# A gated linear recurrence and a feed-forward network: first product in three one-pass products of 12-bit parts, second product plain, one written order for the whole kernel

## The chip, the cores and the metric

The kernel runs on one core of one Trainium2 chip. The metric is the device time of one execution in microseconds (us); the median of several runs is compared. A core has a matrix engine (TensorE, PE in the profile, with its weight loads shown as PEld), VectorE (DVE), ScalarE (ACT), GpSimd (POOL) and a synchronising engine (SP). SP, POOL and ACT also issue DMA transfers. Each engine executes its own instructions in order; between engines semaphores decide who waits.

## The reference, cut to what matters

Float32 throughout. B = 4 batches, H = 8 heads, S = 768 steps, D = 48; 3072 tokens with 384 features; the hidden layer has 2048.

```python
scale = np.minimum(mag, 0.999) / (mag + 1e-06)          # mag = |a_re + i a_im|
for t in range(S):                                      # complex state, one D x D matrix per head
    new_re = ar * S_re - ai * S_im
    new_im = ar * S_im + ai * S_re
    S_re, S_im = (new_re + kv, new_im)                  # kv = outer(k[t], v[t])
    y[:, :, t] = np.einsum('bhd,bhde->bhe', q[:, :, t], S_re)
...
x = attn_out.transpose(0, 2, 1, 3).reshape(B * S, H * D)
h = x @ w_in                                            # (3072 x 384) @ (384 x 2048)
g = h * (1.0 / (1.0 + np.exp(-h)))
return g @ w_out                                        # (3072 x 2048) @ (2048 x 384)
```

## The kernel before

**Tiling.** The 768 steps of a batch are six chunks of 128. The 24 chunks (n = 0 to 23) are taken in 12 pairs (p = 0 to 11), a pair being the same chunk of two batches, so that the feed-forward network sees 256 tokens at a time. Per chunk the recurrence becomes a masked attention: logarithms and angles of the gates (`gates_...`, ACT and DVE), their running sums by a triangular matrix on PE (`phases`, `sums`, line 446 with the operand in two parts of type float32r), sines and cosines (`trig`), decayed and rotated keys and queries (`rotated`, line 540), transposition (`turned`: on PE for n < 4, otherwise 32 x 32 blocks on DVE and twelve DMAs, line 571), scores (`weights`, line 584), mask (`masked`, line 595), output (`output`, lines 614 and 617; lines 651 and 654 for n < 4) and state (`state`, lines 674 and 687). The output is copied to `xT` (line 623, or `put`, line 662, for n < 4).

**Feed-forward network.** Each pair has eight groups jp of 256 hidden units. `hidden` (line 725) makes h for one group: 2 x 3 float32 products of 128 x 128 weights with 256 tokens. `silu` (line 733) applies the activation, PSUM to SBUF. `result` (line 763) multiplies g by `w2`: for p = 0 and 1 plainly, four products of 384 columns per group (line 773); from p = 2 on (`WINO = 2`) by `result_of_halves` (line 790), a scheme with seven products of half size instead of eight (line 817, 192 columns, two hidden blocks at once, so seven per group). That scheme needs sums of the g quarters (`sums_of`, line 760, four DVE operations per group), sums of the weights (`combined`, line 748), and a final step of one ACT copy (line 825) and seven DVE additions (line 829).

**Weights.** The weights arrive as 64-bit floats. `fetch` loads 28 blocks as raw pairs of words (line 191), `high_part` and `convert_low` (lines 47, 49, 224) and `joined` (line 56) turn them into float32 on DVE and ACT, straight into `w1` and `w2`. At the end small pieces of the weights are loaded again and looked at (`small`, line 250, `looked_at`, line 257), which guards a slow path that is not taken here.

**What sets the order.** Pairs 0 to 2 follow a list of tokens written by hand (lines 1020 to 1042); each token is a call, and each engine gets its instructions in the order of the list. In it `h:0` is the first group of `hidden`, `m:..` a mask, `x:0` and `x:1` the copies to `xT` that `h:0` reads. `warm` puts idle matmuls in (line 951). From pair 3 on `step` follows one string (`usual`, lines 1048 and 1049): attention of pair p between the `h` and `r` groups of pair p - 1. Pools rotate their buffers; `kr`, `qr`, `sq`, `part`, `xT`, `y3` (one) and `carry` mostly have two. The DMAs of SP and POOL are issued where the token stands.

Of the kernel before, what the change touches and what calls it, by code (L numbers as in the profile page):

```python
# [30 lines left out]
L_MIN = -60.0  # L31
# [26 lines left out]

@with_exitstack
def kernel(  # L60
# [38 lines left out]
    WINO = 2  # L99
# [5 lines left out]
    ld = fast.enter_context(tc.tile_pool(name="ld", bufs=2))  # L105
    pre = fast.enter_context(tc.tile_pool(name="pre", bufs=1))
    att = fast.enter_context(tc.tile_pool(name="att", bufs=2))
    moe = fast.enter_context(tc.tile_pool(name="moe", bufs=2))
    setup = ExitStack()
    su = setup.enter_context(tc.tile_pool(name="su", bufs=1))  # L110
    conversion = ExitStack()
    cv = conversion.enter_context(tc.tile_pool(name="cv", bufs=1, side="right"))
    later = {}
    startup_psum = ExitStack()
    p_m = fast.enter_context(tc.tile_pool(name="p_m", bufs=2, space=PSUM))
    p_h = fast.enter_context(tc.tile_pool(name="p_h", bufs=2, space=PSUM))
    p_o = startup_psum.enter_context(tc.tile_pool(name="p_o", bufs=4, space=PSUM))
# [20 lines left out]
    def load_a(p, queue=None):  # L138
        for name in ("re", "im"):
            A[p][name] = flat(pre.tile([C, 2, H, D], F32, tag=name, name=f"{name}{p}", bufs=2))  # L140
        for i in range(2):
            b, c = place(2 * p + i)
            for name, ap in (("re", a_re), ("im", a_im)):
                (queue or (nc.gpsimd if p == 0 and i and name == "re" else nc.sync)).dma_start(
                    out=cut(A[p][name], i).rearrange("p (h d) -> p h d", d=D),
                    in_=ap[b].rearrange("h (c p) d -> p c h d", p=C)[:, c])

    def load_x(n, names="kqv", queue=None):
        b, c = place(n)
        for name, ap in zip("kqv", (k, q, v)):  # L150
            if name not in names:
                continue
            if name == "v":

                X[n]["all v"] = ld.tile([C, DM + 64 - D], F32, tag="v", name=f"v{n}", bufs=4)
                nc.gpsimd.memset(X[n]["all v"][:, DM:], 0.0)
                X[n]["v"] = X[n]["all v"][:, 0:DM].rearrange("p (h d) -> p h d", d=D)
            else:
                X[n][name] = ld.tile([C, H, D], F32, tag=name, name=f"{name}{n}", bufs=2)
            (queue or nc.sync).dma_start(  # L160
                out=X[n][name], in_=ap[b].rearrange("h (c p) d -> p c h d", p=C)[:, c])
# [5 lines left out]
    w1 = consts.tile([C, ND, DF], F32)  # L167
# [6 lines left out]
    for s in range(DF // WC):  # L174
        for dc in range(ND):
            blocks.append((w1[:, dc, ts(s, WC)], (1, s), [
                (at, w_in[r:r + n, ts(s, WC)]) for at, r, n in rows_in(H, D, ND, dc)]))
        for j in range(s * WC // C, (s + 1) * WC // C):
            blocks.append((w2[:, j], (2, j // 2), [(0, w_out[ts(j, C)])]))
# [24 lines left out]
    def words(n):  # L204
        if n == len(fetched):
            fetch(1)
        dst, _, parts = blocks[n]
        return dst, fetched[n], parts[0][1].dtype != F32

    def convert_high(n):  # L210
        for _ in range(min(n, len(blocks) - len(highs))):
            dst, raw, does = words(len(highs))
            if does:
                high_part(nc, dst, raw[:, :, 1])
            highs.append(dst)

    def convert_low(n):

        for _ in range(n):
            dst, raw, does = words(len(lows))  # L220
            r = None
            if does:
                r = cv.tile([C, WC], I32, tag="wr", name="r", bufs=3)[:, 0:dst.shape[1]]
                nc.scalar.mul(r, raw[:, :, 0].bitcast(U32), 2.0 ** -29)
            lows.append(r)

    def convert(n):

        for _ in range(min(n, len(blocks) - len(done))):
            if len(done) == len(lows):  # L230
                convert_low(1)
            if len(done) == len(highs):
                convert_high(1)
            dst, r = highs[len(done)], lows[len(done)]
            if r is not None:
                joined(nc, dst, r)
            done.append(dst)

    def converted(which):
        while any(x[1] == which for x in blocks[len(done):]):  # L240
            convert(1)
# [32 lines left out]
    load_a(0)  # L274
# [10 lines left out]
    chained = []  # L285
    by_hand = []
    looks, looked = [], []

    def behind(ins, other):
        tc.add_manual_dep(ins.ins, other.ins.name, mybir.DependencyInfo(  # L290
            mybir.DependencyClass.NoSync, mybir.DependencyReason.DATA))

    def chain(ins):
        if chained and not by_hand:
            behind(ins, chained[-1])
        chained.append(ins)


    def table(of):
        chain(nc.scalar.preload_act_table_set({  # L300
            "exp": "natural_log_exp_and_others", "trig": "trig_and_small",
            "silu": "silu_and_others"}[of]))

    def special(out, in_, func, **kw):
        chain(nc.scalar.activation(out=out, in_=in_, func=func, **kw))  # L305


    def tiles(p, i):

        g = A[p]  # L310
        if "th" not in g:
            for x in ("s1", "s2", "mag"):
                g[x] = flat(pre.tile([C, 2, H, D], F32, tag="t3", name=f"{x}{p}", bufs=5))
            for x in ("l", "th"):
                pool = su if p == 1 else pre
                g[x] = flat(pool.tile([C, 2, H, D], F32, tag=x, name=f"{x}{p}"))
        names = ("re", "im", "s1", "s2", "mag", "l", "th")
        return (g[x] if i is None else cut(g[x], i) for x in names)
# [5 lines left out]
    def squares(p):  # L324
        re, im, s1, s2, _, _, th = tiles(p, None)
# [4 lines left out]
    def gates_square(p):  # L330

        squares(p)
        magnitude(p)

    def magnitude(p):
        re, im, s1, s2, *_ = tiles(p, None)
# [3 lines left out]
    def gates_log(p):  # L340

        re, im, s1, s2, mag, *_ = tiles(p, None)
        special(s1, s1, AF.Ln)
        special(mag, s1, AF.Exp, scale=0.5)
        gates_excess(p)

    def gates_excess(p):
        re, im, s1, s2, *_ = tiles(p, None)
# [3 lines left out]

    def gates_inverse(p):

        re, im, s1, s2, mag, _, th = tiles(p, None)
        nc.vector.tensor_tensor(out=mag, in0=mag, in1=th, op=ALU.add)
        special(mag, mag, AF.Ln)
        special(mag, mag, AF.Exp, scale=-1.0)


    def early_square(i):
        re, im, s1, s2, _, _, th = tiles(0, i)
        special(s1, re, AF.Square)
# [5 lines left out]
    def early_log(i):  # L369

        re, im, s1, s2, mag, l, _ = tiles(0, i)
        special(s1, s1, AF.Ln)
        special(s2, s1, AF.Exp, scale=-0.5)
        nc.vector.tensor_scalar(out=l, in0=s1, scalar1=LN_CAP2, scalar2=0.5, op0=ALU.min,
                                op1=ALU.mult)

    def early_l(i):
        re, im, s1, s2, mag, l, th = tiles(0, i)
        special(s2, s2, AF.Ln, scale=1e-6, bias=one_b)
        nc.vector.tensor_tensor(out=l, in0=l, in1=s2, op=ALU.subtract)  # L380
        special(mag, s1, AF.Exp, scale=0.5)
        nc.vector.tensor_tensor(out=mag, in0=mag, in1=th, op=ALU.add)
        sums(i)

    def early_ratio(i):
        *_, mag, _, _ = tiles(0, i)
        special(mag, mag, AF.Ln)
        special(mag, mag, AF.Exp, scale=-1.0)
# [3 lines left out]
    def gates_l(p, i=None):  # L392

        re, im, s1, s2, mag, l, _ = tiles(p, i)
# [3 lines left out]
    def gates_ratio(p, i=None):  # L398

        re, im, s1, s2, mag, l, _ = tiles(p, i)  # L400
# [834 lines left out]
```

## Time and profile before

| What | us |
|---|---|
| three runs | 657.31, 653.33, 656.92 |
| median | 656.92 |
| span of the profiled execution | 655.6 |
| first matmul of the first feed-forward product (line 725) starts | 45.98 |
| one pair in the steady part (for instance 303.46 to 353.70) | 50.24 |
| last matmul starts, end of the span | 651.08, 655.6 |

The profiled execution lies inside the three runs, 1.3 us under their median. "Busy" of PE is the union of matmul intervals whose ends are modelled; consecutive matmuls overlap, so what one costs is read from the distance between starts. A float32 product stands as two matmul records in the profile (1152 records of line 725 for 12 x 8 x 6 = 576 products).

| Row of the profile | records | mean ns of one |
|---|---|---|
| line 725, first product, 256 columns | 1152 | 380 |
| line 773, second product plain, 384 columns | 128 | 489 |
| line 817, second product by halves, 192 columns, all four forms together | 1120 | 326 to 332 |
| line 760, sums of g quarters, DVE | 320 | 283 to 292 |
| line 829, last additions, DVE | 70 | 352 |
| line 305, silu, ACT, 128 x 512 | 96 | 596 |
| ACT table loads, lines 300 and 305 | 84 | 1283 |

### The profile page before, as it was taken

To read this page: it belongs to the slowest core of one execution; us is meant where nothing else is said; L and a number is where in the kernel's file an instruction comes from. 1 tells how busy PE (TensorE), PEld (TensorE's weight loads), DVE (VectorE), ACT (ScalarE), POOL (GpSimd) and SP (SyncE) were. 2 spreads that over 40 slices of the span, in tenths; PEclk is the share of its full clock that TensorE was granted. 3 is DMA by queue.
4 is the path that set the end of the run, shared out by engine and by line. 5 is a ranking of instruction groups with operands and counts; after the bars stand their busy time and mean duration, and the time that the engine had idled before them with its cause. 6 is when DMAs were issued, how large, how long until landed. Compare 5 with 4: busy or idle time off the path is not lost.

```text
span 655.6 us, 11519 instructions
## 1 busy us (share of the span) xinstructions
PE 634.7 (97%) x4084; PEld 562.1 (86%) x4084; DVE 468.4 (71%) x1009; ACT 367.2 (56%) x537; POOL 213.8 (33%) x368
## 2 busy tenths in 40 slices
PE   5789999999999999999999999999999999998997
PEld 4668866777999999999999999999999999987997
DVE  5898379847975885885895894894894895864543
ACT  6798599796852852762762672672681681410110
POOL 7436000370342334334334334234244240140000
PEclk9899999999999999999999999999999999998999
DMA  9878465583393394394295296187187183678640
GB/s 168 173 189 171 113 178 126 117 134 86 47 153 49 61 146 62 56 139 73 47 141 79 41 135 91 35 122 109 31 125 110 32 116 56 201 160 226 204 141 27
DMA packets 183445, 73.28 MB, mean 112 GB/s; under 512 B 166224, under 2 KB 171816, under 8 KB 183384
## 3 DMA queue, kind: packets, MB, share of 16 engines
q1 hardware_dynamic: 168424, 50.79, 39.5%
q0 software_dynamic: 11648, 17.20, 17.1%
q10 hardware_dynamic: 3312, 4.52, 1.9%
q8 instruction: 33, 0.54, 0.4%
q14 instruction: 28, 0.23, 0.1%
HBM read 48.90 MB, written 4.79 MB: 82 GB/s over the span
## 4 chain that ended last, share of the span: by engine, by line
PE 80%; ACT 7%; DVE 5%; DMA 4%; SPq 2%; issue 1%; DVEq 0%; ACTq 0%
PE h L725 32%; PE o L817 27%; PE a L584 6%; PE y L614 3%; PE o L773 3%; PE y L617 3%; DMA raw<-in_moe_w_in_dram 2%; PE s L687 2%; ACT L305 2%; SPq L571 1%; PE phase L446 1%; ACT mag L305 1%; ACT s L305 1%; PE L L446 1%; DMA im<-in_a_im_dram 1%
## 5 line engine op out<-in xcount | busy, mean ns | idle before, releaser
L725 PE MATMUL h<-xT,w 128*128 128x256 f32 x1152 | 260.6, 380 | 0.0
L725 PEld LDWEIGHTS h<-xT,w 128*128 128x128 f32 x1152 | 216.4, 190 | 29.2
L305 ACT ACTIVATE g<-h 128x512 f32<-128x512 f32 x96 | 55.3, 596 | 140.3 <-PE h L725 133.2
L571 POOL DMA_DIRECT2D T<-sq x120 | 77.5, 653 | 71.9 <-issue 56.0
L517 POOL DMA_DIRECT2D dec<-ends x48 | 30.8, 648 | 154.9 <-DMA ends<-eq 154.9
L300 ACT ACT_TABLE_LOAD x62 | 79.5, 1283 | 2.0 <-PEq L1219 0.9
L817 PE MATMUL o<-w,gs 128*128 128x192 f32 x320 | 77.8, 326 | 0.0
L699 POOL DMA_DIRECT2D S<-ssq x84 | 45.8, 553 | 94.8 <-DVE ssq L691 56.5
L595 DVE TENSOR_TENSOR w<-a,upto_r 128x512 f32<-128x512 f32 x48 | 32.9, 687 | 53.5 <-PE a L584 53.5
L817 PE MATMUL o<-w,g 128*128 128x192 f32 x320 | 67.2, 332 | 0.0
L817 PE MATMUL o<-wc,gs 128*128 128x192 f32 x320 | 64.9, 326 | 0.0
L623 ACT COPY xT<-y 128x384 f32<-128x384 f32 x20 | 9.6, 478 | 98.1 <-PE y L617 98.1
L817 PEld LDWEIGHTS o<-w,g 128*128 128x128 f32 x320 | 54.0, 191 | 4.5 <-issue 2.0
L817 PEld LDWEIGHTS o<-w,gs 128*128 128x128 f32 x320 | 56.3, 190 | 0.0
L584 PEld LDWEIGHTS a<-T 96*128 96x128 f32 x384 | 49.4, 191 | 7.6 <-issue 3.5
L584 PE MATMUL a<-T 96*128 96x128 f32 x384 | 51.3, 276 | 3.7 <-DMA T<-sq 2.5
L817 PEld LDWEIGHTS o<-wc,gs 128*128 128x128 f32 x320 | 54.2, 190 | 0.0
L760 DVE TENSOR_TENSOR gs<-g 128x128 f32<-128x128 f32 x160 | 38.6, 283 | 20.4 <-PE o L817 13.9
L773 PE MATMUL o<-w,g 128*128 128x384 f32 x128 | 43.7, 489 | 0.8 <-ACT g L305 0.8
L817 PE MATMUL o<-wc,g 128*128 128x192 f32 x160 | 38.9, 326 | 0.0
L773 PEld LDWEIGHTS o<-w,g 128*128 128x128 f32 x128 | 23.8, 190 | 16.7 <-ACT g L305 1.8
L614 PE MATMUL y<-w,v 128*64 128x128 f32 x320 | 36.0, 287 | 0.0
(123 smaller groups left out, 987.3 us busy)
## 6 DMA issues: line engine op xcount, KB each, us to landing
T<-sq SPq DMA_DIRECT2D x120, 64.0 KB
T<-sq POOLq DMA_DIRECT2D x120, 64.0 KB, 4.1
raw<-in_moe_w_out_dram SPq DMA_DIRECT2D x16, 384.0 KB
small<-in_moe_w_in_dram SPq DMA_DIRECT2D x16, 384.0 KB
small<-in_moe_w_out_dram SPq DMA_DIRECT2D x16, 384.0 KB
raw<-in_moe_w_in_dram SPq DMA_DIRECT2D x24, 192.0 KB
out_dram<-ot ACTq DMA_DIRECT2D x23, 192.0 KB
im<-in_a_im_dram SPq DMA_DIRECT2D x16, 192.0 KB
```

What stands on the lines that cost most here:

```text
L300: chain(nc.scalar.preload_act_table_set({"exp": "natural_log_exp_and_others", "trig": "trig_and_small", "silu": "silu_and_others"}[of]))
L305: chain(nc.scalar.activation(out=out, in_=in_, func=func, **kw))
L517: nc.gpsimd.dma_start(out=x["dec"][a * D:(a + 1) * D], in_=ends[n].rearrange("(h d) -> d h", d=D))
L571: (nc.gpsimd if a % 2 else nc.sync).dma_start(out=to[ts(b, Q), :, a], in_=sq[ts(a, Q), b])
L584: nc.tensor.matmul(ps[:, h], lhsT=x["kT"][:, hh * HH + h], rhs=x["qT"][:, hh * HH + h], start=True, stop=True)
L595: nc.vector.tensor_tensor(out=x["w", hh], in0=x["a", hh], in1=upto.unsqueeze(1).to_broadcast([C, HH, C]), op=ALU.mult)
L614: nc.tensor.matmul(to, lhsT=v_[:, cols], rhs=x["w", h // HH][:, h % HH], start=True, stop=not carried)
L699: (nc.gpsimd if g % 2 else nc.sync).dma_start(out=to[ts(b, Q), r, :, e], in_=sq[ts(g, Q), :, b, 0:e.stop - e.start])
L725: nc.tensor.matmul(ps[:, ji], lhsT=w1[:, dc, ts(jp * 2 + ji, C)], rhs=A[p]["xT"][:, dc], start=(dc == 0), stop=(dc == ND - 1))
L760: nc.vector.tensor_tensor(out=t[:, i], in0=a, in1=b, op=op)
L773: nc.tensor.matmul(A[p]["o"][m].rearrange("p n c -> p (n c)"), lhsT=A[p]["g", jp][:, ji, ts(m, C)], rhs=w2[:, j], start=(j == 0), stop=(j ...
L817: nc.tensor.matmul(o[i], lhsT=a, rhs=b, start=(jp == 0 and i < 4), stop=(final and j == jp and i in ((5, 3, 6, 2) if p == NP - 1 else (4, ...
```

## The change

From pair 3 on (`SPLIT = 3`) the first product is made from parts. With x = xa + xb and w = wa + wb, where xa and wa hold the upper 12 significant bits (`head`: the lower 12 bits are cleared) and the tails xb and wb the rest, two products of type float32r are accumulated in one PSUM tile, u = wa xa + 4096 wb xb, and a third is made in another, v = (wa - 4096 wb)(xa - 4096 xb). Then h = (1 + 2^-12) u - 2^-12 v: ACT writes -KAPPA v to g, DVE adds u, and `silu` takes g in place with the scale 1 + 2^-12. The second product is plain for all pairs; `sums_of`, `combined` and `result_of_halves` are gone.

New data: the tails of `w1` (`tails`), the rounded heads written back into `w1` itself, and the sums, which are stored to DRAM (`w_kept`) and loaded for each group and each pair (`w_loaded`, 128 x 3 x 256 words of four bytes, two buffers). The 12 blocks of `w_in` are converted in a small tile `wt` and moved to `w1` by a DMA (`move`), since `w1` is now a float32r tile.

The list of tokens now covers the whole kernel, pairs 0 to 11; `step` and `usual` are gone. All pools are wrapped in `Ring`, which takes buffers in strict turn; `kr`, `qr`, `sq`, `part`, `xT` and `carry` have one buffer. Activation tables are loaded where a function isn't in the loaded set, and the sine may come from the set that has silu. Loads of a, k, q and v are separate tokens, on POOL when marked g. In the built program ACT has 72 table loads in place of 84.

```diff
+    SPLIT = 3
+    KAPPA = 2.0 ** -12 / (1 + 2.0 ** -12)
-    w1 = consts.tile([C, ND, DF], F32)
+    w1 = consts.tile([C, ND, DF], F32R)
+    w1f = w1.bitcast(F32)
...
+    def move(g):
+        n, src = moved.pop(0)
+        queue_of(g).dma_start(out=blocks[n][0].bitcast(I32), in_=src.bitcast(I32))
...
     def hidden(p, jp):
+        if p >= SPLIT:
+            hidden_of_parts(p, jp)
+            return
...
+    def head(dst, src):
+        nc.vector.tensor_scalar(out=dst.bitcast(I32), in0=src.bitcast(I32), scalar1=-4096,
+                                scalar2=None, op0=ALU.bitwise_and)
+    def difference(dst, tail, whole):
+        nc.vector.scalar_tensor_tensor(out=dst, in0=tail, scalar=-4096.0, in1=whole,
+                                       op0=ALU.mult, op1=ALU.add)
+    # per block of w1: w_head, w_tail, w_sum (DVE), w_scaled, w_rounded (ACT), w_kept (two DMAs)
+    # per pair: x_head, x_tail, x_sum (DVE), x_rounded (ACT)
+    def w_loaded(p, jp):
+        t = A[p]["w sum", jp] = room("right").tile([C, ND, 2 * C], F32R, tag="w_sum",
+                                                   name=f"ws{p}_{jp}", bufs=2)
+        nc.sync.dma_start(out=t.bitcast(I32), in_=second_d[jp].bitcast(I32))
+    def hidden_of_parts(p, jp):
+        v = late_h().tile([C, 2, T], F32, tag="hv", name=f"hv{p}_{jp}")
+        u = p_h.tile([C, 2, T], F32, tag="h", name=f"hu{p}_{jp}")
+        x = A[p]
+        for ji in range(2):
+            for dc in range(ND):
+                nc.tensor.matmul(v[:, ji], lhsT=x["w sum", jp][:, dc, ts(ji, C)],
+                                 rhs=x["xs"][:, dc], start=(dc == 0), stop=(dc == ND - 1))
+        for ji in range(2):
+            for dc in range(ND):
+                cols = ts(jp * 2 + ji, C)
+                nc.tensor.matmul(u[:, ji], lhsT=w1[:, dc, cols], rhs=x["xa"][:, dc],
+                                 start=(dc == 0), stop=False)
+                nc.tensor.matmul(u[:, ji], lhsT=tails()[:, dc, cols], rhs=x["xb"][:, dc],
+                                 start=False, stop=(dc == ND - 1))
+    def second_scaled(p, jp):
+        g = A[p]["g", jp] = moe.tile([C, 2, T], F32, tag="g", name=f"g{p}_{jp}", bufs=4)
+        nc.scalar.mul(g, A[p]["v", jp], -KAPPA)
+    def h_joined(p, jp):
+        g = A[p]["g", jp]
+        nc.vector.tensor_tensor(out=g, in0=g, in1=A[p]["u", jp], op=ALU.add)
...
     def result(p, jp):
-        if p >= WINO:
-            result_of_halves(p, jp)
-            return
...
-    usual = ("c h E h kA qA h r tA D kB h L qB r F h tB wA wB r G h A X a0A th uA uB h a1A r sA h a0B yA "
-             "r a1B sB r pA yB pB mA S r mB r lA lB")
```

The two comment lines in the diff stand for one-line functions. The new list begins like this, up to the first group of `hidden` (H, R and J convert a weight block on DVE, ACT and DVE; G0 to Ga are the gates of the pair after the colon; m is a mask, y an output, x a copy to `xT`):

```
im:0 warm:30 re:0 re:1g hold: im:1 F: F: e0:0 e1:0 re:2g re:3g e2:0 e3:0 e0:1 e1:1
e4:0 e2:1 e6:0 warm:34 e4:1 im:2g im:3g e7:0 q:0g e3:1 e6:1 v:0g e5:0 e8:0 e7:1
e8:1 at:0.1 k:1g warm:20 H: G0:1 H: G5:1 k:0g q:1g L:0 an:0.1 phase:1 v:1g at:0.0
R: G8:1 exp:0 an:0.0 phase:0 turn:1 J: turn:0 G1:1 e5:1 L:1 G7:1 G2:1 im:4g im:5g
G3:1 re:4g re:5g G4:1 dk:0 ends:0 G6:1 G9:1 thirds:1 dq:0 trig:0 trig:1 L:2 F:
im:6g G0:2 F: exp:1 M: last:1 v:4g Ga:1 phase:2 rq:0.0 rq:0.1 H: exp:2 H: turn:2
v:3g rk:0.0 last:0 carry:4 F: R: im:7g rk:0.1 s:0 G5:2 F: dk:1 G8:2 dq:1 S:0 G1:2
q:2g re:6g J: ends:2 M: R: R: R: J: M: G7:2 t:0.2 t:0.3 t:0.1 rq:1.1 T:0.3 T:0.2
T:0.1 t:0.0 w:0.1 rq:1.0 ends:1 rk:1.1 t:1.1 rk:1.0 k:3g t:1.0 s:1 T:0.0 m:0.1
thirds:0 w:0.0 last:2 H: G3:2 G6:2 G9:2 J: R: F: t:1.3 k:2g t:1.2 J: H: dq:2 J:
T:1.3 T:1.1 m:0.0 T:1.2 w:1.1 Ga:2 y:0 L:3 S:1 m:1.1 R: F: F: F: trig:2 rq:2.0
T:1.0 w:1.0 m:1.0 y:1 H: H: v:2g R: x:0 x:1 dk:2 phase:3 exp:3 R: F: h:0.1
```

## The prediction, made before the result was known

> **What bounds the kernel now.** I read the page's busy table and slices first, then the chain of work that ended last, then the busy time by stretch, then timelines of PE.
>
> ```profile
> span 655.6 us, 11519 instructions
> PE 634.7 (97%) x4084; PEld 562.1 (86%) x4084; DVE 468.4 (71%) x1009; ACT 367.2 (56%) x537; POOL 213.8 (33%) x368
> ...
> PE   5789999999999999999999999999999999998997
> ...
> PE 80%; ACT 7%; DVE 5%; DMA 4%; SPq 2%; issue 1%; DVEq 0%; ACTq 0%
> ```
>
> PE is the bound, except in the first three slices, where it is 50 to 80% busy. By stretch (columns: stretch, length, PE, PEld, DVE, ACT, POOL busy with counts, clock, DMA share, GB/s):
>
> ```profile
> 0.00:46.00 46.00, 33.31 (x245) 25.04 (x246) 34.78 (x66) 35.38 (x60) 27.14 (x50) 0.96 0.82 175
> 303.46:353.70 50.24, 50.24 (x346) 46.43 (x346) 37.74 (x84) 27.57 (x40) 18.59 (x34) 1.00 0.59 88
> ```
>
> In the steady part PE has no idle time at all, so a pair costs the sum of its matmuls. At the start PE waits: the first h group begins at 45.98, and the PE work ahead of it (84 idle matmuls, four sums and phases, two chunks of attention) adds up to about 30 us, so some 16 us are lost. What the matmuls cost shows in the timeline (start, extent, count):
>
> ```profile
> 584.79 2.76 PE L725 MATMUL h<-xT,w 128*128 128x256 f32 x12
> 302.62 0.81 PE L817 MATMUL o<-wc,gs 128*128 128x192 f32 x4
> 56.38 2.75 PE L773 MATMUL o<-w,g 128*128 128x384 f32 x8
> 13.18 3.88 PE L951 MATMUL idle<-upto_r 128*128 128x256 bf16 x34
> 299.75 0.72 PE L584 MATMUL a<-T 96*128 96x128 f32 x5
> 310.68 0.49 PE L817 MATMUL o<-w,gs 128*128 128x192 f32 x2
> 310.87 1.00 PE L446 MATMUL L<-l_parts,half_r 128*128 128x384 f32 x4
> 311.71 0.81 PE L725 MATMUL h<-xT,w 128*128 128x256 f32 x3
> ```
>
> An extent is (count - 1) distances plus one duration. Line 725: (2.76 - 0.38)/11 = 0.216 us a record; line 817: (0.81 - 0.326)/3 = 0.162; line 773: (2.75 - 0.489)/7 = 0.323; the idle bf16 matmul: (3.88 - 0.32)/33 = 0.108. Line 446 is the one float32r product here, one record for each: line 817 occupies PE to 310.68 + 2 x 0.162 = 311.00, the next matmul of line 725 starts at 311.71, so four float32r products of 384 columns take 0.71, 0.177 each.
>
> [...] two records of 0.216 us a product, 0.432, are four times the 0.108 of bf16. [...] the 128-column scores at (0.72 - 0.275)/4 = 0.111 us a record are near that.
>
> **The change, part by part.** The sum is made against 655.6 and carried to the median of 656.9.
>
> *PE, first product.* From pair 3 on, nine pairs x 8 groups x 18 float32r products of 256 columns = 1296. No such product is in the trace. [...] I take the middle of these two, 0.121, and keep 0.112 to 0.124.
>
> *PE, sum.* Before: 1152 x 0.216 + 128 x 0.323 + 1120 x 0.162 = 248.8 + 41.3 + 181.4 = 471.5. After: three pairs 288 x 0.216 = 62.2, second product 12 x 64 x 0.323 = 248.1, and 1296 x 0.121 = 156.8; 467.1. So **-4.4 us**: the parts gain 186.6 - 156.8 = 29.8, the lost halves method costs 25.4. With 0.112 it is -16, with 0.124 -0.5. Attention, sums and idle matmuls are the same in number.
>
> *DVE and ACT later on.* DVE loses lines 760 (84.8 us), 829 (21.5) and 748 (7), and gains 72 joins of 128 x 512 like line 595 (0.687, 49.5), 12 weight blocks (0.47 + 0.69 + 0.69 each, 22) and nine pairs' x parts (0.59 + 0.95 + 0.95 each, 22): 19 us less. ACT gains 72 scalings (0.6, 43), 12 blocks at 1.28 (15), x parts (0.84, 8), copies of the result, and loses 12 table loads (15.4). Against PE's 50 us a pair both keep 10 us free; I cost this at nothing; if the cover is gone, PE waits for g.
>
> *The start.* This is the largest step. In the new order's DVE queue more work stands ahead of the fourth mask (`m:1.0`), without which `y:1`, `x:1` and the first h group can't be: three w_out blocks (3 x 1.46), pair 2's gates (0.93 + 0.59 + 0.96 + 0.95 + 1.92), the turn and half the decay and rotation of chunk 2 (2.2) and pair 1's angle (1.9, after the masks before): 13.9 us. On DVE the starts lie 0.08 us closer than the durations (two 128 x 512 masks take 1.28, not 1.37, below), so 12.6 us. ACT has 12.4 us more ahead of `x:1` (seven table loads in place of five, pair 2's squares and logarithms, weight blocks).
>
> ```profile
> 6.44 0.56 DVE L364 TENSOR_TENSOR s<-im 128x384 f32<-128x384 f32 x1 [5.38 <-DMA im<-in_a_im_dram]
> ...
> 41.03 1.28 DVE L595 TENSOR_TENSOR w<-a,upto_r 128x512 f32<-128x512 f32 x2
> ```
>
> DVE starts at 6.4 and ends the fourth mask at 42.3 with 4.8 us of waits between. If the added work fills all of these, the first h group is 7.8 us later, if none, 12.6. I take **+10**. Nothing can fill PE's wait: all its work before the first h group is in both orders. Later masks and g's of pairs 0 to 2 stand less far behind PE than this one, so the delay is paid once. The queues: POOL has five a loads ahead of `q:0` (0.9 us each), SP the moves and more raw blocks, 7 to 11 fetched by then; DMA is already at a share of 0.82. I put this inside the +10 as DVE's queue is the longer one; ACT's and the DMAs' excess belongs to the upper end.
>
> *The loads of the sums.* 72 DMAs of 384 KB on SP, three rows of 1 KB a partition in one piece, with an issue of about 0.33 us like line 250's; 24 stores and 12 moves besides. SP issues ahead, unless its head waits: a load waits for the first six products of the group two before. From there to its own group the PE work in between is 4.0 us at least; for 8 of 70 loads under 5, for 11 under 6, for 22 under 8. [...] If loads land 5 us after the release, PE waits 4.6 us in all, with 4 us 0.1. I take **+2**. Moving parts to one buffer (`kr`, `qr`, `sq`, `part`, `xT`) adds waits of DVE and ACT, hidden by the same 10 us a pair; 0, at most a few us.
>
> *The end.* The last matmul starts 4.5 us before the end; after it now come two copies and stores of 192 KB in place of copy, additions and stores: 0, within 1 us.
>
> **Sum:** 656.9 - 4.4 + 10 + 2 = **664.5 us**, +1.2%. Its own range, with 0.119 and 0.124, 7.8 and 12.6, 0 and 4.6: 657 to 673.
>
> **The rivals.** *Faster products (other side):* [...] PE gains 16 us; with the smaller delay at the start, 656.9 - 16.1 + 7.8 = 649. For: the scores' 0.111. [...] It decides below 0.114. *The start costs nothing*, since DVE's waits and better loads give back what was put ahead: 656.9 - 4.4 = 652.5. Against: the queue is in order. *PE waits for the sums:* SP's head is blocked by a chunk's transposition DMAs (twelve issues took 13.07 us on SP in the steady part), loads land 6 us after the release, 14.9 us in all: 656.9 - 4.4 + 10 + 14.9 = 677. For: DMA share 0.59 before, and eight loads a pair come on top. Against: the lead is planned at 4 us or more. *It isn't one pass:* float32r at two records' cost, 0.216: +119 us. Against: line 446 has one record a product, at 0.177 for 384.
>
> **How the numbers follow.** A measurement here can tell about 1% from no change (650.3 to 663.5). Likeliest case 0.52 (a third of it under 663.5), faster products 0.20, no cost at the start 0.10, waits for the sums 0.16, not one pass 0.02. Faster 0.22, same 0.29, slower 0.49. Range 647 to 678.
>
> **What would show it.** Right: 1296 float32r records 0.12 us apart; the first h group at 53 to 59 us, with PE idle before it and DVE busy; no PE idle in the steady part; a pair there about 49 us. Wrong: the first h group before 50; a spacing under 0.114 or over 0.13; PE waits put down to `w_sum` DMAs or to T.

## The result, and the profile after

The changed kernel is slower: 684.79 us, the median of four runs (684.47 to 688.34), against 657.12 (653.33 to 657.43) for the kernel before on the same chip. The ratio is 1.046, with a 95% interval of 1.041 to 1.051. The profiled execution has a span of 682.6 us, 27.0 above that of before.

The page of the changed kernel, the same parts as shown of before:

```profile
span 682.6 us, 11681 instructions
...
PE 634.1 (93%) x4036; PEld 493.6 (72%) x4036; DVE 452.0 (66%) x750; ACT 419.0 (61%) x640; POOL 215.4 (32%) x368
...
PE   6379989999999998989999999999899999999993
...
PEclk9569999999999999999999999999999999999997
DMA  9988984652565889664979985889778745574685
...
PE 63%; DMA 16%; DVE 9%; ACT 4%; SPq 4%; issue 2%; POOL 0%; DVEq 0%; ACTq 0%; POOLq 0%
```

PE's share of the chain of waits fell from 80% to 63% and DMA's rose from 4% to 16%: the kernel now waits for transfers. The second and third slice show a clock of 0.5 and 0.6, and in its last slice PE is busy for only three tenths. Two stretches of the busy table, up to the first group of the first product and the stretch shown of before (stretch, length, PE, PEld, DVE, ACT, POOL busy with counts, clock, DMA share, GB/s):

```profile
0.00:59.02 59.02, 38.84 (x245) 28.40 (x246) 45.82 (x85) 46.95 (x74) 30.52 (x53) 0.77 0.94 184
303.46:353.70 50.24, 50.24 (x347) 40.64 (x346) 34.84 (x56) 36.47 (x56) 16.56 (x31) 1.00 0.71 142
```

The same number of matmuls (245) takes 59.02 us instead of 46.00, at a clock of 0.77 and with the DMA engines busy for 94% of the time. Later the DMA share is 0.71 instead of 0.59.

The float32r product, one record each, is as fast as was hoped. Part of PE's timeline (start, extent):

```profile
303.11 0.28 PE L826 MATMUL hu<-xa,w 128*128 128x256 f32 x1
303.23 0.28 PE L828 MATMUL hu<-xb,tails 128*128 128x256 f32 x1
303.35 0.28 PE L826 MATMUL hu<-xa,w 128*128 128x256 f32 x1
303.46 0.28 PE L828 MATMUL hu<-xb,tails 128*128 128x256 f32 x1
```

The starts are 0.12 us apart; over all records of lines 826 and 828 the median distance is 0.118.

But PE waits in other places. In the costliest groups (busy, mean ns, then idle time before and what ended most of it):

```profile
L821 PE MATMUL hv<-xs,ws 128*128 128x256 f32 x432 | 71.3, 301 | 7.2 <-DMA ws<-w_sums 7.0
L266 DVE TENSOR_REDUCE tiny<-small 128x1 f32<-128x384 f32 x32 | 17.2, 548 | 31.9 <-DMA small<-in_moe_w_in_dram 17.9
```

Line 821 is the first product of a group, which reads the loaded sums. Line 266 is the reduction that looks at the weights. The end of the kernel shows it late:

```profile
660.75 10.48 PE L849 MATMUL o<-w,g 128*128 128x384 f32 x32
...
673.01 0.55 DVE L266 TENSOR_REDUCE tiny<-small 128x1 f32<-128x384 f32 x1 [3.11 <-DMA small<-in_moe_w_out_dram]
...
675.65 0.55 DVE L266 TENSOR_REDUCE tiny<-small 128x1 f32<-128x384 f32 x1 [0.52 <-DMA small<-in_moe_w_out_dram]
...
678.63 0.30 DVE L1079 TENSOR_REDUCE weak<-all__6492 1x1 int32<-1x152 f32 x1 [2.02 <-DMA all__6492<-fit]
```

PE's last matmul starts at 670.75. Four reductions of the look start after that, with three waits for loads among them, and the final comparison stands behind them: 11.9 us pass from the last matmul to the end, where before had 4.5.

**Where the 27.0 us lie.** I counted every distance between matmul starts that is more than 0.25 us above the median of its kind (line and shape of the earlier matmul) as a gap. Up to 102 us the gaps are 27.2 us (before 11.9), after that 22.9 (before 4.2), and the end is 11.9 (before 4.5). These are 41.4 us more. All distances without the gaps add up to 618.5 us instead of 631.6, so PE's own work is 13.0 us less, and the first matmul starts 1.3 us earlier; that is the whole difference. In the middle 8.4 us in six gaps are put down to the loads of sums and 5.5 to DVE (`l_parts`, `th_parts`, `g`); 7.6 us more lie in 24 gaps, all but one of 0.3 us, for which the profile names no cause.

### The profile page after: what moved, and what is told of

Same layout as the page of the kernel before. It is cut to its first block, busy times and chain, and to the rows that moved or that the text cites. A ratio compares the mean times of both kernels' runs of the same rounds, so it can differ in the third digit from the quotient of the medians.

```text
span 682.6 us, 11681 instructions
## 1 busy us (share of the span) xinstructions
PE 634.1 (93%) x4036; PEld 493.6 (72%) x4036; DVE 452.0 (66%) x750; ACT 419.0 (61%) x640; POOL 215.4 (32%) x368
## 4 chain that ended last, share of the span: by engine, by line
PE 63%; DMA 16%; DVE 9%; ACT 4%; SPq 4%; issue 2%; POOL 0%; DVEq 0%; ACTq 0%; POOLq 0%
PE o L849 24%; PE hv L821 7%; PE h L727 6%; PE hu L826 6%; PE hu L828 6%; PE a L583 5%; DMA raw<-in_moe_w_in_dram 4%; DMA ws<-w_sums 4%; PE y L610 2%; DMA small<-in_moe_w_out_dram 2%; PE y L613 2%; DMA small<-in_moe_w_in_dram 2%; PE s L681 1%; SPq L203 1%; ACT L300 1%
## 5 line engine op out<-in xcount | busy, mean ns | idle before, releaser
L849 PE MATMUL o<-w,g 128*128 128x384 f32 x768 | 257.5, 487 | 0.7 <-ACT g L306 0.7
L849 PEld LDWEIGHTS o<-w,g 128*128 128x128 f32 x768 | 142.8, 190 | 89.3 <-ACT g L306 1.1
L826 PE MATMUL hu<-xa,w 128*128 128x256 f32 x432 | 106.6, 283 | 1.2 <-DVE g L838 1.2
L828 PE MATMUL hu<-xb,tails 128*128 128x256 f32 x432 | 106.2, 282 | 0.0
L517 POOL DMA_DIRECT2D dec<-ends x48 | 31.2, 655 | 176.2 <-DMA ends<-eq 170.1
L826 PEld LDWEIGHTS hu<-xa,w 128*128 128x128 f32 x432 | 81.8, 189 | 1.8 <-DVE g L838 1.6
L828 PEld LDWEIGHTS hu<-xb,tails 128*128 128x128 f32 x432 | 82.1, 190 | 0.0
L821 PE MATMUL hv<-xs,ws 128*128 128x256 f32 x432 | 71.3, 301 | 7.2 <-DMA ws<-w_sums 7.0
L821 PEld LDWEIGHTS hv<-xs,ws 128*128 128x128 f32 x432 | 58.1, 190 | 17.3 <-DMA ws<-w_sums 5.8
L727 PE MATMUL h<-xT,w 128*128 128x256 f32 x288 | 65.4, 381 | 1.1 <-DMA w<-wt 1.1
L727 PEld LDWEIGHTS h<-xT,w 128*128 128x128 f32 x288 | 53.9, 190 | 10.8 <-DMA w<-wt 1.5
L591 DVE TENSOR_TENSOR w<-a,upto_r 128x512 f32<-128x512 f32 x48 | 32.6, 684 | 26.4 <-PE a L583 24.9
```

The source lines that it names most:

```text
L727: nc.tensor.matmul(ps[:, ji], lhsT=w1f[:, dc, ts(jp * 2 + ji, C)], rhs=A[p]["xT"][:, dc], start=(dc == 0), stop=(dc == ND - 1))
L821: nc.tensor.matmul(v[:, ji], lhsT=x["w sum", jp][:, dc, ts(ji, C)], rhs=x["xs"][:, dc], start=(dc == 0), stop=(dc == ND - 1))
L826: nc.tensor.matmul(u[:, ji], lhsT=w1[:, dc, cols], rhs=x["xa"][:, dc], start=(dc == 0), stop=False)
L828: nc.tensor.matmul(u[:, ji], lhsT=tails()[:, dc, cols], rhs=x["xb"][:, dc], start=False, stop=(dc == ND - 1))
L849: nc.tensor.matmul(A[p]["o"][m].rearrange("p n c -> p (n c)"), lhsT=A[p]["g", jp][:, ji, ts(m, C)], rhs=w2[:, j], start=(j == 0), stop=(j ...
```

## The experiments

All times are medians of three rounds or more; ratios are to the kernel before on the same chip, which lay between 654.0 and 657.1 us. "First group" is the start of line 727, and "tail" the time from the start of the last matmul to the end, both of the profiled execution.

| run | us | ratio (95%) | first group | last matmul | tail |
|---|---|---|---|---|---|
| before | 657.1 | | 46.0 | 651.1 | 4.5 |
| after | 684.8 | 1.046 (1.041 to 1.051) | 59.0 | 670.7 | 11.9 |
| before_plain | 676.3 | 1.032 (1.027 to 1.037) | 43.6 | 668.5 | 4.9 |
| parts_left_out | 699.6 | 1.065 (1.058 to 1.071) | 57.4 | 694.4 | 4.6 |
| no_weight_check | 675.8 | 1.030 (1.025 to 1.036) | 58.8 | 670.1 | 4.6 |
| sums_loaded_once | 674.4 | 1.030 (1.023 to 1.036) | 57.8 | 660.7 | 12.1 |
| no_check_sums_once | 666.8 | 1.016 (1.011 to 1.022) | 57.8 | 661.9 | 5.1 |
| weight_check_earlier | 711.3 | 1.083 (1.076 to 1.091) | 58.1 | 708.2 | 4.6 |
| check_on_gpsimd_queue | 697.0 | 1.064 (1.056 to 1.071) | 57.1 | 690.4 | 4.6 |
| check_by_groups | 684.7 | 1.045 (1.038 to 1.052) | 58.4 | 679.7 | 4.6 |
| sums_two_and_a_half_ahead | 689.8 | 1.053 (1.048 to 1.059) | 57.5 | 682.5 | 4.6 |

### What the two products are worth

In before_plain the kernel before gets a plain second product and nothing else:

```diff
-        if p >= WINO:
-            result_of_halves(p, jp)
-            return
... (and the calls that make its sums)
```

> The kernel before with the second product plain from pair 2 on too (sums_of, the combined weights and the last additions are gone), order unchanged. Theory: PE has no idle time there, so 10 pairs x (64 x 0.323 - 112 x 0.162) = 25.3 us come on top: 682. Rival: the DVE operations that go (113 us in all) gave PE hidden waits, so that less comes on top: under 678.

It came at 676.3, 3.2% or 21 us above before. The loss is some four us smaller than the 25.4 of the sum. The time lies where the rival put it, but the rival's reason covers only a part: PE's gaps are 1.4 us shorter here, while the distances of the second product (lines 773 and 817 before) grew by 21.7 us instead of 25.4.

In parts_left_out the changed kernel keeps its order, but all pairs use the plain first product. The tokens that make and load the parts are dropped, the activation stands where the join stood, and `xT` and `g` have more buffers:

```diff
-    SPLIT = 3
+    SPLIT = 12
...
```

> The changed kernel in its own order, but with the first product plain in all pairs: the three products of parts, the making of the parts of weights and rows, and the loads of sums are left out. It tells what the parts bring net. TensorE: 72 groups at 2.59 instead of 2.12 us are 33.7 more. Theory A, that the loads of sums (10 us by the run sums_loaded_once) and VectorE's work on the parts (4 to 6 us of gaps put down to it) are the only prices: 684.8 + 33.7 - 15 = 701 to 705. Theory B, that the order itself makes the waits: 712 to 719. Rival: the parts' prices eat most of their gain: below 695.

It came at 699.6: a little under theory A. By the ratios (1.065 to 1.046) the parts bring only 12 us net, by the medians 15, of the 33.7 that the spacing gives (72 groups, 12 x 0.216 less 18 x 0.118 each). In the two profiles the matmul distances of the changed kernel are 36.1 us shorter than here, but its gaps after 102 us are 13.7 us longer and its tail 7.3. The look at the weights has the same tokens in both; here its last reduction is over at 677, while PE runs to 694.4 and covers it. Against before_plain the new order, with its buffers, costs 3.2%, 21 us, while all products are the same. Some of that may belong to the run itself: 7.0 us of its gaps after 200 us are waits for the activation, which stands elsewhere here than in either kernel. The first group is late in it too, at 57.4 against 43.6: so neither the parts nor the plain product make the start late.

### The end: the look at the weights

```diff
-        for x in """ ... sm:0 ... lk:0 ... """.split():
+        for x in """ ... (all sm: and lk: tokens left out) ... """.split():
```

> The changed kernel without the 32 loads and reductions that look at small pieces of the weights (the guard of the slow path is left out; the output stays the same). Theory: in the changed kernel these loads come so late that the end waits for them (12 us from the last matmul's start to the end, against 4.5 in the kernel before). Then about 7.5 us go, 677, and the end is 4 to 5 us after the last matmul's start. Rival: the end is late because of the stores or the last copies; then within 1 us of 684.8. If the loads of the sums also suffered from these loads in the last pairs, 1 to 3 us more.

It came at 675.8 with a tail of 4.6: the look costs 9 us by the medians, 10 by the ratios, and 7.3 us of that is tail. The next three runs keep the look and only move it. First, spread evenly from the last pair's gates on:

> The changed kernel with the 32 loads and 32 reductions of the weights' look spread evenly from the last gates of the last pair to the middle of the last pair's groups, four loads ahead of the reductions; nothing is left out. Theory: the end is late only because these stand too close to the end; last matmul to end falls from 11.9 to 4 to 5 us, and the time to 676 to 679 (675.8 without them at all). Rival: their 12.6 MB and VectorE time then delay the groups of the last two pairs by as much: 681 to 686.

The tail fell to 4.6, but the time rose to 711.3. What SP waited for from 540 to 660 us (in all, times, longest):

```profile
SPq L259 <- DVE tiny L266: 54.5, 16, 6.4
```

SP stood for 54.5 us with a load of the look at its head, until DVE had emptied the buffer. Line 813, the load of sums, is on the same queue behind it, and PE's gaps put down to these loads are 26.4 us in this run, against 8.4. So the loads were put on another queue:

```diff
-            nc.sync.dma_start(
+            nc.gpsimd.dma_start(
                 out=raw.bitcast(I32), in_=w[:, ts(n % (NT // 2), DM)].bitcast(I32).rearrange(
```

> As the run weight_check_earlier (711.3), with the 32 loads of the look on GpSimd's queue instead of SyncE's; nothing is left out. Theory: there the loads of the look waited 54 us on SyncE's queue for their buffers, and the loads of sums stood behind them; on another queue both go their way, and the time is 675 to 680, as without the look (675.8). Rival: it is the bandwidth or VectorE's reductions: 695 or more.

This missed: 697.0, 14 us better than on SP, 12 worse than after. PE's gaps put down to the loads of sums fell to 9.1 us, so the part about SP's queue held. The time itself lies in the rival's range, and bandwidth isn't excluded. But now GpSimd's queue was held. What it waited for from 540 to 640 us:

```profile
POOL small L259 <- DVE tiny L266: 50.1, 17, 6.5
```

Half of the transfers `T<-sq` stand on that queue, and one of PE's gaps, 7.1 us at 595.8, was put down to them. A longer one, 8.3 us at 552, was put down to the copy of a result (`ot`), for which the profile names a transfer `S<-ssq` as the last wait, also on that queue. The third try leaves a whole group between a reduction and the load that takes its buffer:

> The changed kernel with the look's loads two at a time at the groups of the first product from the last gates on, each pair of reductions a group behind its loads and a group ahead of the loads that take the same buffers; still on SyncE's queue; nothing is left out. Theory: weight_check_earlier and check_on_gpsimd_queue were long because a load of the look stood at the head of its queue until VectorE had emptied its buffer, with the loads of sums, or the transposed blocks, behind it. With a group between them no queue is held: last matmul to end 4 to 6 us, time 675 to 680. Rival: the loads themselves are too much beside those of the sums: 686 or more.

SP's waits for `tiny` are 13.6 us in this run and 15.7 in after, and the time is 684.7, the same as after and between theory and rival. The tail is 4.6, but the last matmul starts 8.9 us later: what the end gained was lost ahead of it. From 550 to 600 us, check_by_groups:

```profile
550.00:600.00 50.00, 46.90 (x316) 37.91 (x317) 35.78 (x62) 21.72 (x38) 7.95 (x13) 1.00 0.82 246
```

and the changed kernel:

```profile
550.00:600.00 50.00, 50.00 (x326) 39.46 (x324) 31.87 (x52) 20.53 (x38) 9.92 (x17) 1.00 0.55 140
```

The DMA engines are at 0.82 instead of 0.55 and move 246 instead of 140 GB/s, and PE has 3 us of holes. Over the whole run the gaps put down to loads of sums are 13.0 us in eight, against 8.4 in six. And a gap can cost more than its length, as one did here. PE in check_by_groups:

```profile
291.31 0.51 PE L451 MATMUL L<-l_parts,half_r 128*128 128x384 f32 x2
294.20 1.52 PE L821 MATMUL hv<-xs,ws 128*128 128x256 f32 x6 [2.38 <-DMA ws<-w_sums]
295.52 0.41 PE L826 MATMUL hu<-xa,w 128*128 128x256 f32 x1
295.74 0.41 PE L828 MATMUL hu<-xb,tails 128*128 128x256 f32 x1
295.95 0.41 PE L826 MATMUL hu<-xa,w 128*128 128x256 f32 x1
```

After a wait of 2.38 us the distance is 0.21 instead of 0.12, up to 297.5; the busy table gives a clock of 0.54 for 294.0 to 297.5. By an estimate from these distances the stretch cost about 1.5 us (16 distances, 0.09 longer each). check_by_groups has one more before it, with a clock of 0.53 for 260 to 263; the changed kernel has a single one between its start and its last matmul, at 0.50 from 489.6 to 493.0. The two in check_by_groups fall where nothing of the look is, so they can't be put down to the look itself; the run shows no more than that moving the look brought no gain.

### The loads of the sums

In sums_loaded_once only the first two of the 72 loads are made, and all later groups use these two tiles:

```diff
+        same = later.setdefault("same sums", [])
+        if len(same) == 2:
+            A[p]["w sum", jp] = same[jp % 2]
+            return
```

> The changed kernel with two of the 72 loads of the weight sums; all other groups use these two tiles (70 loads left out, so the first product is wrong from pair 3 on; the instructions of PE, DVE and ACT are the same). Theory: PE's waits put down to these loads (about 8 us between 200 and 560) and some of the waits that other transfers cause go: 684.8 - 8 to -15, 670 to 677. Rival: the waits only change their name, since the DVE and SP queues are late on their own account: 682 or more. If nothing else hid behind the loads, the end stays 12 us after the last matmul's start.

674.4: the loads cost 10.4 us by the medians, 10.6 by the ratios, where the gaps put down to them are 8.4. Between the two profiles, whose spans differ by 9.8, the gaps after 102 us are 8.6 shorter and the distances without gaps 3.7 shorter, 1.5 of it the half-clock stretch, while the gaps before 102 us are 2.3 longer. The tail is unchanged at 12.1, so the loads of sums aren't what makes the look late. Both left out:

> The changed kernel without the look at the weights (as no_weight_check, -9.0) and with the sums loaded only twice (as sums_loaded_once, -10.4); both are left out together. If the two are separate prices: 684.8 - 19.4 = 665, 663 to 668. If they are one price seen twice (loads that stand in each other's way): 670 to 675.

666.8, 18.0 below after and by the ratios 19: two separate prices, which add. Even so the kernel is 1.6% above before. Whether more buffers would help was tried on top of check_by_groups, with half tiles in a ring of five:

```diff
-        t = ... .tile([C, ND, 2 * C], F32R, tag="w_sum", name=f"ws{p}_{jp}", bufs=2)
-        nc.sync.dma_start(out=t.bitcast(I32), in_=second_d[jp].bitcast(I32))
+        for ji in range(2):
+            t = room("right").tile([C, ND, C], F32R, tag="w_sum", name=..., bufs=5)
+            nc.sync.dma_start(out=t.bitcast(I32), in_=second_d[jp * 2 + ji].bitcast(I32))
```

> check_by_groups, with each group's sums in two tiles of 192 KB in a ring of five, instead of one of 384 KB in a ring of two; nothing is left out. Theory A, that the loads come late because there are only two buffers: 3 to 6 us below check_by_groups. Theory B, that the DMA engines are full in these stretches: within 1.5 us of check_by_groups, or slower.

689.8, 5 us slower; theory A falls for this form. The number fits theory B, but its reason isn't shown: the run also has twice as many stores and loads of sums on SP's queue. For the same reason it doesn't tell what a third whole buffer would do, which wasn't tried.

### The start

| run | us | first group | PE gaps to 102 us |
|---|---|---|---|
| after | 684.8 | 59.0 | 27.2 |
| gates_later | 704.3 | 57.6 | 37.7 |
| weight_blocks_later | 694.5 | 65.7 | 31.2 |
| start_of_before | 697.8 | 53.7 | 35.5 |
| start_kept_warm | 688.8 | 59.5 | 15.2 |
| gates_later_and_warm | 702.4 | 56.7 | 26.5 |
| gates_later_warm_ends_early | 706.0 | 62.0 | 27.6 |
| start_rebuilt | 709.4 | 60.5 | 30.3 |
| parts_left_out_no_move | 695.7 | 58.3 | 26.1 |

In gates_later, pair 2's gates, dq:2, trig:2, rq:2.0 and three blocks of `w_out` with their fetches stand behind h:0.0.

> The changed kernel with the work that stands ahead of the first feed-forward group without being needed for it (gates of pair 2, three output weight blocks, part of chunk 2's rotation) moved behind that group, on all engines; nothing else. Theory: the start is set by DVE's queue, so the first h group, at 59.0 in the changed kernel, comes 8 to 10 us earlier, and the whole is 6 to 10 us shorter, 675 to 679. Rival 1: the start is set by the DMAs (their share there is 0.92), then the first group comes at 56 or later and the whole gains under 3 us. Rival 2: the moved work is late afterwards; then the first group is early, but PE waits between 60 and 100 us and the whole gains nothing.

A miss. The first group came only 1.4 us earlier, though DVE is busy for 35.9 us ahead of it instead of 45.8, about as in before (34.8). So the amount of DVE's work doesn't explain the late start. And PE waited 16.3 us right afterwards for line 670: its `kr` stood on DVE behind the postponed gates and weight blocks until 79.0 us. Next only the first two weight blocks (F, H, R, J, M) were moved back.

> The changed kernel, with only the first two weight blocks' fetches, conversion and move put behind the first ends (about where the kernel before has them); nothing is left out. Theory: at the start VectorE's queue is held by the high half of the first weight block, which waits for a load that takes 11.7 us, so the angle of pair 0 and the phase products come late: the first phase product then starts near 16 us instead of 22, the first group of the first product at 52 to 55 us instead of 59.0, and the time is 677 to 681 against 684.8. Rival: the start is set by the loads' bandwidth or by later waits; the first group stays at 57 to 59 us and the time at 683 to 687.

Worse. DVE's timeline in this run shows what the edit brought in:

```profile
32.95 0.69 DVE L49 SCALAR_TENSOR_TENSOR wt<-raw,wt 128x512 int32<-128x512 int32 x1
35.30 0.69 DVE L56 CUSTOM_DVE_ANT_0 wt<-wt,r 128x1024 uint16<-128x1024 uint16 x1 [1.66 <-ACT r L236]
41.95 0.43 DVE L47 TENSOR_SCALAR wt<-raw 128x512 int32<-128x512 int32 x1 [5.96 <-DMA w<-wt]
```

With two `wt` buffers the third block waits for the first one's move, and everything behind it on DVE waits too: PE had a gap of 13.8 us. In start_of_before the whole list up to the first group is that of before, with the leftover tokens behind it; both_repairs adds the spread look.

> The changed kernel with the start list of the kernel before up to the first two groups of the first product, and behind it the changed list as it is; nothing is left out. Theory: the new order of the start costs 13 us; the first group then stands at 46 to 50 us instead of 59.0, and the time at 672 to 677 against 684.8. Rival: what was taken earlier (gates of pair 2, weight blocks) only moves behind, and opens gaps there, as in the run gates_later: first group at 46 to 50, but the time at 682 to 700.

> The start of the kernel before and the look spread earlier, together; nothing is left out. Theory, that start and end add: 684.8 - 9 - 8 = 665 to 670, still above the 657 of before by the waits for sums and for VectorE. Rival: the waits in the middle shrink with the start (fewer loads bunched up), then below 660; or the start's work comes back as gaps, 674 or more.

The rival's times held in both: 697.8 (first group at 53.7, then a gap of 16.0 us at 58.7) and 722.7. But even with the list of before the first group came later than the 46 to 50 us that theory and rival had. The next run asks whether the clock makes the start long; 101 idle products fill PE's gaps.

> The changed kernel with 101 more of its idle bf16 products in the gaps of TensorE between 14 and 38 us; nothing is left out. Theory A, the start is set by VectorE, which works without a hole from 20 to 58 us: the clock rises from 0.68 to above 0.9 in this stretch, and the first group stays at 57 to 59 us, the time at 682 to 686. Theory B, the low clock is what makes the start long: first group at 53 to 56 us, time 678 to 682.

From 20 to 60 us the clock is 0.79 here and 0.68 in after:

```profile
20.00:60.00 40.00, 32.78 (x207) 24.68 (x208) 38.22 (x68) 33.23 (x52) 16.69 (x25) 0.79 0.91 190
```

The first group stays at 59.5, with DVE busy for 38.2 of 40 us, as theory A has it; the clock rose less than it expected. The time is wide (682.7 to 692.5), and its median of 688.8 lies above both ranges. Then gates and clock together:

> The idle products of start_kept_warm, and the gates of pair 2 with dq, trig and rq of chunk 2 (about 13 us of VectorE) moved behind h:0.0; the weight blocks stay where the changed kernel has them; nothing is left out. If both VectorE and the clock hold the start, the first group comes at 49 to 54 us, against 57.7 in gates_later; if loads of weights do, it stays at 56 to 58. The gates are then due at once, so the whole time says little: 680 to 695.

Still 56.7. Here the chain of waits shows what came up next (start, extent, what):

```profile
42.95 2.31 DMA ends<-eq
...
46.42 6.13 DMA dec<-ends
...
52.64 0.55 DVE S L716
53.19 1.21 DVE w L591 x2
```

The last decays of chunk 1 go to DRAM and come back, and DVE's queue has the state update ahead of the last masks. Two runs tried to get round this, the first by an earlier write, the second also with four groups ahead of the postponed gates.

> gates_later_and_warm (first group 56.7, 702.4), with the write of chunk 1's last decays put behind its exponential, ahead of the first move of a weight block; nothing is left out. There the chain of waits went, from 42.7 us on, through SyncE's queue, this write, its load back as dec (6.1 us) and VectorE's update of the state, with the masks behind it. If this round trip is what is late next, the first group comes at 51 to 54 us; if yet another wait stands behind it, at 55 to 57. The whole time says little: 695 to 705.

> As gates_later_warm_ends_early, and the four groups of pair 0 up to h:0.2 with the weight blocks that they need put ahead of the postponed gates, so that TensorE has 18 us of work while VectorE makes the gates; nothing is left out. If the 13 us of the start are a matter of order alone, they come back in part: first group at 51 to 54 us and a time of 674 to 681. Rival, that VectorE's and the loads' work of the first 100 us is due anyway, wherever it stands: 684 to 700.

Both missed, with first groups at 62.0 and 60.5 us. In start_rebuilt PE again waited 14.4 us at 74.3 for DVE's `kr`. Last, the move of weight blocks, tried without the parts, where `w1` can stay float32:

> parts_left_out (699.6), with the blocks of the first weight converted in their place, as in the kernel before, instead of in a buffer from which a DMA moves them; left out is what parts_left_out leaves out. Theory A, the moves hold the start: first group at 48 to 54 us instead of 57.4, time 690 to 695. Theory B, the order of the queues does: first group at 56 to 58 us, time 697 to 701.

The first group stays at 58.3, so the moves don't hold it. The time is 3.9 us below parts_left_out, but the intervals of the two ratios overlap (1.056 to 1.066, 1.058 to 1.071).

So the start is not settled. No one of the gates, the clock and the moves holds it alone, and every order I wrote was slower than the one given. What the two profiles show is that in the first 100 us the changed kernel gives DVE 80.7 us of work instead of 70.9 and moves 19.9 MB instead of 16.3 (busy time and rates by stretch). That fits the rival that this work is due anyway, but isn't proof of it. The transfers ahead of the first group remain a candidate of their own: 10.1 to 11.0 MB in the runs where it comes at 56.7 us or later, 8.5 in start_of_before (53.7) and 8.1 in before (46.0). A later group also leaves more time for transfers, and no run moved them alone.

## Why the prediction was wrong

Slower was the likeliest of the three directions; the time was outside the range, +27.7 against +7.6.

| term of the sum | predicted | measured |
|---|---|---|
| PE, all matmuls | -4.4 | -13.0 (distances without gaps) |
| of it first product | -29.8 | -33.7 by the spacing of 0.118 |
| of it second product plain | +25.4 | +21 (before_plain) |
| start, paid once | +10 | first group +13.0; gaps up to 102 us +15.3 |
| loads of sums | +2 | +10 (sums_loaded_once) |
| DVE and ACT later | 0 | 5.5 in gaps put down to DVE |
| end | 0, within 1 | tail +7.4; the look costs +9 to +10 (no_weight_check) |

- **PE's sum held.** The spacing of 0.118 fell inside 0.112 to 0.124. That range was my estimate, since before has no float32r product of 256 columns, and what sets the spacing no run shows. PE's own work fell by 13.0 us, more than the 4.4. The change does on TensorE what it says.
- **The start had the right sign and nearly the right size**, with +13.0 just above 7.8 to 12.6. Two things under it failed. "The delay is paid once" failed in part: from the first group to 102 us PE has another 4.5 us of gaps, against 0.9 before. And the reason given, the length of DVE's queue, isn't enough: with most of that work gone the first group moved by 1.4 us only. So the size was right partly by luck.
- **The loads of sums** were the term most mis-sized of those that were priced. The step that failed is "SP issues ahead, unless its head waits". The planned lead held: from the last product that read a buffer to the group that needs it again, 6 of 70 loads had under 5 us, 14 under 6 and 21 under 8. The landing held too: the sums were there 4.0 us after the issue in the median (2.9 to 8.1), where 5 us from the release were allowed, and the loads of this size in before (line 250) took 3.0 to 5.9. But the issue came late: for 16 of the 70 loads more than 5 us after the buffer was free, at most 13.2. One of them (SP's issues, then PE's wait):

```profile
353.98 6.78 SPq L571 DMA_DIRECT2D T<-sq  x6
...
361.38 0.33 SPq L813 DMA_DIRECT2D ws<-w_sums  x1
...
364.83 0.99 PE L821 MATMUL hv<-xs,ws 128*128 128x256 f32 x6 [1.28 <-DMA ws<-w_sums]
```

The buffer was free at 348.4. SP issued what stood ahead in its queue until 361.4 (its waits for semaphores in this time add up to 1.0 us), the sums were there at 364.8, and PE waited 1.28 us. In the four waits of 0.8 us or more the issue came 2.5 to 12.9 us after the release and the landing 3.4 to 5.9 us after the issue; by an estimate from these numbers, issued at the release all four would have been in time. This was the mechanism of the rival with 14.9 us, SP's queue blocked by transfers, and not a slow landing. No run moved the loads of sums to another place or queue, so it is read from the trace and not tested. Not priced at all was the slow clock behind a wait (0.50 from 489.6 to 493.0).
- **The end** failed outright. I looked at the stores behind the last matmul, but not at the look, which must be over too before the last comparison. Most of its tokens stand among the last of the new list: its last load was issued at 670.3 us, 12.3 us before the end, where before had issued it 26.1 us before the end.
- **"Both keep 10 us free a pair"** failed in part: it was a mean over a pair, while from 239 to 289 us DVE is busy 45.4 of 50 us.

With the look and the loads both left out (no_check_sums_once) the time is 666.8, and the prediction without its term for the loads is 662.5: these two terms carry most of the miss. That the rest comes so near is in part luck, since the larger gain on PE (13.0 for 4.4) hides more gaps at the start and behind DVE.

The signs that were named worked: 1296 records at 0.12, the first group at the edge of 53 to 59, and under "wrong", PE waits put down to the sums. The two cases of "faster" were both refuted: a spacing under 0.114, and a start at no cost.

## What to carry to other kernels

A change that saves matmul time and adds transfers has to price their place in the issuing queue, not only their landing: here loads landed 4.0 us after issue, as planned, but SP issued them up to 13.2 us after their buffers were free, and a term of 2 us became 10. Follow every chain to the last instruction of the program, not only the one behind the last matmul. And in a list written by hand, where work waits for what stands ahead of it on its queue (16.3 us of PE for a `kr` in gates_later), a few tokens moved can cost more than they free (the seven of weight_blocks_later 10 us), so an edit has to name what stands behind it on each queue it passes.

## What the runs showed of the hardware that was not expected

Behind a PE wait of little more than 2 us the clock was halved. In the changed kernel the wait was 2.19 us:

```profile
488.51 0.97 PE L821 MATMUL hv<-xs,ws 128*128 128x256 f32 x6 [2.19 <-DMA ws<-w_sums]
...
489.92 0.42 PE L826 MATMUL hu<-xa,w 128*128 128x256 f32 x1
490.14 0.41 PE L828 MATMUL hu<-xb,tails 128*128 128x256 f32 x1
```

The distance between the last two is 0.22 us, where the median of the run is 0.118. A longer wait in the same run, for the same loads, had no such stretch behind it:

```profile
292.57 0.95 PE L821 MATMUL hv<-xs,ws 128*128 128x256 f32 x6 [2.52 <-DMA ws<-w_sums]
...
293.36 0.28 PE L826 MATMUL hu<-xa,w 128*128 128x256 f32 x1
293.47 0.28 PE L828 MATMUL hu<-xb,tails 128*128 128x256 f32 x1
```

Three us behind each of the two, from the busy table (the column before the last two is the clock, PE's busy time is the first after the length):

```profile
489.70:492.70 3.00, 3.00 (x17) 3.00 (x16) 0.00 (x0) 0.42 (x1) 0.70 (x2) 0.50 0.62 123
292.60:295.60 3.00, 3.00 (x27) 3.00 (x27) 1.00 (x2) 1.88 (x2) 0.00 (x0) 1.00 0.15 24
```

So the clock was 0.50 behind the wait of 2.19 us and 1.00 behind the one of 2.52: the length of the wait alone doesn't tell whether the slow stretch follows, and what does was not shown. The kernel before has a case too: a wait of 2.13 us for `T<-sq` up to 595.44, and a clock of 0.50 from 597.0 to 600.4.
